# Head sums of batches 4 to 7 on ScalarE's accumulator, exponent clamps of the output weights on GpSimd

## The chip, the cores and the metric

The kernel runs on one core of a Trainium2 chip. A core has a matrix engine (TensorE, PE in the profile, with PEld for its weight loads), VectorE (DVE), ScalarE (ACT), GpSimd (POOL) and SyncE (SP), which here only starts transfers. Each engine takes its own instructions strictly in the order in which the program issues them, and waits at an instruction until its inputs and its output buffer are free. The metric is the device time of one execution in microseconds, as the median of several executions; lower is better.

## The reference

The inputs `q`, `k`, `v` have the shape 8 x 8 x 576 x 64 (batch, head, token, head width) in float32; the three weights arrive as float64. Attention without a softmax gives `x`, and a gated unit with a causal convolution of 5 taps over the tokens gives the output:

```python
kv = np.einsum('bhsd,bhse->bhde', k, v)
out = np.einsum('bhsd,bhde->bhse', q, kv)
rms = np.sqrt(np.mean(out * out, axis=-1, keepdims=True) + 1e-06)
x = out / rms * g_norm            # then (B, S, H*D): 8 x 576 x 512
gate = 1 / (1 + np.exp(-sum over 5 taps of conv_w * shifted x))
result = (gate * (x @ w_val)) @ w_out
```

What matters here is the root mean square: for each token and each head the 64 values of `out` are squared and summed, and the value is then scaled by the sum to the power of -1/2.

## The kernel before

**Order.** The order of the work is written out by hand. `PLAN` (lines 19 to 204) is a list of steps, each a function name with its indices, and lines 816 to 818 call them one after the other. Since each engine works in order, the order of the steps in `PLAN` is the order of every engine's queue, SP's and POOL's transfer queues among them. A step named later can run earlier only if it is on another engine. All eight batches are pipelined against each other: while batch b is normalised, batch b-1 goes through the gate and the value product, and batch pair (b-2)/2 through the output product.

**Batches and chunks.** A batch has 576 tokens, cut into four chunks of 128 tokens (`c` = 0 to 3) and a tail of 64 (`c` = 4). A chunk has 8 heads on 128 partitions; the tail is laid out as 4 head columns on 128 partitions. A step `square 4 1` is chunk 1 of batch 4.

**The path of one chunk, batches 1 to 7.** `raw_pair` (PE) writes the attention output of two chunks into PSUM banks (`raw`, line 501). `square` (ACT, line 535) squares it with two instructions for one chunk, of four heads each, into one of two `sq` buffers in SBUF, whose rows have a 65th column that holds 64 times epsilon. `sums` (DVE, line 544) reduces the 65 columns of each head to `ss`. `powers` (POOL, line 552) raises `ss` to -1/2 and writes `rt`. `normalise` (ACT, line 571) reads `raw` once more and scales it head by head with 8 instructions of 64 columns. `turn_blocks` (DVE) and `move_blocks` (transfers issued by POOL and SP) turn it into `xT`; the tail goes through `turn_x` (PE) and `keep_x` (ACT, line 590).

**What else is in ACT's queue.** `gate_start` (line 615) and `gate_end` (line 628) stand around the four `gate_tap` steps of DVE (line 621). The value product `val_fast` (PE, line 682) writes bank `va`, `vb` or `vc`; `val_keep` with a last index of 0, 1, 2 or 6 (ACT, lines 691, 693, 695, 703) and of 3, 4, 5 (DVE, line 689) copies or adds the bank to `gv`. Indices 0, 2, 4, 6 of `val_fast` all go to the same bank `va`, so `val_fast b m 2` can't start on PE before `val_keep b m 0` has left ACT; index 5 goes to the bank that `val_keep` 1 reads. The output product `fast_product` (PE, line 774) and `fast_keep` (ACT lines 786, 788, 790, 797; DVE line 784) are built in the same way. There are eight PSUM banks, given out in turn. Two lines of `PLAN` show how closely it is woven (the steps on ACT here are `square`, `gate_start`, `val_keep` 0 and 2):

```python
    fast_product 0 3 6; gate_start 3 2; square 4 1; load_q 5 0; load_half k 5 0; square 4 0; turn_blocks 4 2;
    fast_keep 0 3 5; x_sums 3 2; sums 4 0; sums 4 1; val_keep 3 1 0; gate_end 2 3; val_fast 3 1 2; gated 2 3;
```

**The weights.** `narrow_weight` turns float64 into float32 in eight steps per weight piece: step 0 (DVE, line 363) takes the exponent out of the high word into `e`; steps 1, 2 and 3 (ACT, lines 368, 370 and 372) shift it by 896 and clamp it to 0 to 255, place it at bit 23; step 4 (DVE, line 375) adds the sign; steps 5, 6 and 7 (DVE) handle the mantissa and multiply. `wout` has four pieces of 128 x 512, in the order 1, 0, 2, 3.

Of the kernel before, what the change touches and what calls it, by code (L numbers as in the profile page):

```python
# [9 lines left out]
FP32 = mybir.dt.float32  # L10
U32 = mybir.dt.uint32
AF = mybir.ActivationFunctionType
ALU = mybir.AluOpType
AX = mybir.AxisListType

P = 128
EPS = 1e-6
# [190 lines left out]
def kernel(  # L208
# [11 lines left out]
    nc = tc.nc  # L220
    B, H, S, D = q.shape
    C = H * D
    HP = H // 2
    NJ = S // P
# [11 lines left out]
    SV = S // NV  # L236
    ACT_NORM = range(1, B)
    WHOLE = (0,)
    TURNED_X = 2
    FAST_VAL = 2  # L240
    FAST_OUT = 0
# [8 lines left out]
    work = ctx.enter_context(tc.tile_pool(name="work", bufs=2))  # L250
# [18 lines left out]
    wout = const.tile([P, NK, C], FP32, name="wout")  # L269
# [26 lines left out]
    st = {}  # L296
# [51 lines left out]
    def narrow(key, dst, n):  # L348


        w = staged[key]
        rows, size = w.shape[0], w.shape[1]
        split = lambda a: a if len(dst.shape) == 2 else a.rearrange(
            "p (m c) -> p m c", m=dst.shape[1])
        lo, hi = w[:, :, 0], w[:, :, 1]
        if n in (0, 5, 6):
            tag, kind, bufs = {0: ("wexp", U32, 2), 5: ("ot", U32, 3), 6: ("ot", FP32, 3)}[n]
            staged[key, n] = work.tile(
                [P, C], kind, tag=tag, bufs=bufs, name=f"{tag}{n}_{key[0]}{key[1]}")[0:rows, 0:size]
        e, m, mf = (staged.get((key, part)) for part in (0, 5, 6))  # L360

        if n == 0:
            nc.vector.tensor_scalar(
                out=e, in0=hi, scalar1=20, scalar2=0x7FF,
                op0=ALU.logical_shift_right, op1=ALU.bitwise_and,
            )
        elif n == 1:
            nc.scalar.activation(out=e, in_=e, func=AF.Relu, bias=biases[0:rows, 0:1])
        elif n == 2:
            nc.scalar.activation(out=e, in_=e, func=AF.Relu, bias=biases[0:rows, 1:2], scale=-1.0)  # L370
        elif n == 3:
            nc.scalar.activation(
                out=e, in_=e, func=AF.Identity, bias=biases[0:rows, 2:3], scale=-float(1 << 23))
        elif n == 4:
            nc.vector.scalar_tensor_tensor(
                out=e, in0=hi, scalar=0x80000000, in1=e, op0=ALU.bitwise_and, op1=ALU.bitwise_or,
            )
        elif n == 5:

            nc.vector.tensor_scalar(  # L380
                out=m, in0=hi, scalar1=0xFFFFF, scalar2=1 << 20,
                op0=ALU.bitwise_and, op1=ALU.bitwise_or,
            )
        elif n == 6:
            nc.vector.scalar_tensor_tensor(
                out=mf, in0=lo, scalar=2.0 ** -32, in1=m, op0=ALU.mult, op1=ALU.add,
            )
        else:
            nc.vector.scalar_tensor_tensor(
                out=dst, in0=split(mf), scalar=gcol[:] if key[0] == "wval" else 2.0 ** -20,  # L390
                in1=split(e.bitcast(FP32)),
                op0=ALU.mult, op1=ALU.mult,
            )
# [15 lines left out]
    def narrow_weight(*key):  # L409
        narrow(key[0:2], weights[key[0:2]][3], key[2])  # L410
# [34 lines left out]
    def kv_copy(b, s):  # L445
        ps_ = st["kvps", b][s]
        if b in WHOLE:
            for r in range(2):
# [73 lines left out]
    def heads(c):  # L522
        return H if c < NJ else H // 2

    FIRST = {3: 0, 2: H, 4: 2 * H, 1: 2 * H + H // 2, 0: 3 * H + H // 2}

    def square(b, c):
        n = heads(c)
        sq = st["sq", b, c] = sqs[(b * (NJ + 1) + list(FIRST).index(c)) % len(sqs)]
        if b in WHOLE:  # L530
            nc.scalar.activation(  # L531
                out=sq[:, 0:n, 0:D], in_=st["raw", b, c][:].rearrange("p (h e) -> p h e", e=D), func=AF.Square)
            return
        for r, raw in enumerate(st["raw", b, c]):
            nc.scalar.activation(  # L535
                out=sq[:, r * n // 2:(r + 1) * n // 2, 0:D], in_=raw.rearrange("p (h e) -> p h e", e=D),
                func=AF.Square)

    def sums(b, c):
        if ("ss", b) not in st:  # L540
            for name in ("ss", "rt"):
                st[name, b] = work.tile([P, NJ * H + H // 2], FP32, tag=name, bufs=2, name=f"{name}{b}")
        n = heads(c)
        nc.vector.reduce_sum(  # L544
            out=st["ss", b][:, FIRST[c]:FIRST[c] + n], in_=st["sq", b, c][:, 0:n], axis=AX.X)

    def root_range(b, c):
        return slice(FIRST[c], FIRST[c] + ROOTS.get((b, c), heads(c)))

    def powers(b, c):  # L550
        which = root_range(b, c)
        nc.gpsimd.tensor_tensor(  # L552
            out=st["rt", b][:, which], in0=st["ss", b][:, which], in1=mhalf[:, which], op=ALU.pow)

    def normalise(b, c):
# [3 lines left out]
        root = st["rt", b][:, FIRST[c]:FIRST[c] + n]  # L559
        if b in WHOLE:  # L560
            nc.vector.tensor_tensor(
# [240 lines left out]
    def store(i, c, queue=nc.sync, blocks=range(HB)):  # L802
# [5 lines left out]
    steps = {f.__name__: f for f in (  # L808
        load_half, load_q, load_q_rows, stage_weight, narrow_weight, turn_cw, keep_cw, start_warm, warm_up,
        kv_product, kv_copy, turn_q, turn_q_rows, sort_q, raw_whole, raw_pair, raw_tail, square, sums, powers, normalise,  # L810
        turn_x, keep_x, turn_blocks, move_blocks, halo, gate_start, gate_tap, gate_end, val_product, keep_val, gated,
        val_sums, x_sums, val_fast, val_keep, out_product, keep_out, weight_sums, token_sums, fast_product, fast_keep,
# [36 lines left out]
```

## Time and profile before

| What | Value |
|---|---|
| Time, median of 3 runs | 304.34 us (303.98 to 304.76) |
| Span of the profiled execution | 304.6 us |
| PE busy, share of the span | 294.8 us, 97% |
| DVE busy | 269.2 us, 88% |
| ACT busy | 193.7 us, 64% |
| POOL busy | 114.9 us, 38% |

The span is that of one execution, which the page of the profile describes; it agrees with the runs to 0.1%, and no other time is given for this execution. An engine is busy while it executes; matmuls are pipelined, so a busy PE is not PE at its peak. Instructions on ACT overlap at their ends, so the busy time of a group divided by its count is less than the mean duration of one. The timeline of the trace names lines of the kernel; which batch and chunk an instruction belongs to follows by counting, since each line runs in the order of `PLAN`.

### The profile page before, as it was taken

Reading aid. Unit: us, or ns where it says so; the run is one execution under the profiler, and the core shown is the slowest. Engines: PE = TensorE matmul, PEld = TensorE weight load, DVE = VectorE, ACT = ScalarE, POOL = GpSimd, SP = SyncE. Lnnn points to the kernel's source line nnn. Section 1 sums busy time; section 2 is a strip of 40 time slices with the busy share of each in tenths; the row PEclk is TensorE's granted clock in tenths of the full one; section 3 lists DMA queues with packets and bytes.
Section 4 is the critical chain, followed back from the end, with each engine's and each line's share of the span. In section 5 each row is a group of like instructions: output and inputs, shape, how many; then the busy total and the mean of one; then the engine's idle time right before and its main releaser. Section 6 shows DMA issues by size and latency. Waiting matters only on the chain.

```text
span 304.6 us, 8977 instructions
## 1 busy us (share of the span) xinstructions
PE 294.8 (97%) x3441; PEld 232.4 (76%) x3441; DVE 269.2 (88%) x474; ACT 193.7 (64%) x596; POOL 114.9 (38%) x127
## 2 busy tenths in 40 slices
PE   7899999999999999999999999999999999999993
PEld 7788778877787785777778757787878588888582
DVE  1169999999999999999999999999999999999612
ACT  1569989999768664884586547683787354535220
POOL 3027354406568217364338352345536631000000
PEclk9979999999999999999999999999999999999999
DMA  7999998088569756988689477927411621112423
GB/s 269 343 368 343 272 302 210 4 230 269 154 147 329 231 163 167 269 220 260 173 253 294 111 175 232 326 72 214 114 48 30 169 80 34 36 42 64 103 69 103
DMA packets 32074, 55.53 MB, mean 182 GB/s; under 512 B 6166, under 2 KB 14358, under 8 KB 32032
## 3 DMA queue, kind: packets, MB, share of 16 engines
q1 hardware_dynamic: 29520, 49.76, 55.7%
q0 software_dynamic: 1632, 3.17, 4.1%
q10 hardware_dynamic: 880, 2.03, 1.8%
q8 instruction: 27, 0.44, 0.6%
q14 instruction: 15, 0.12, 0.1%
HBM read 39.21 MB, written 9.44 MB: 160 GB/s over the span
## 4 chain that ended last, share of the span: by engine, by line
PE 89%; DVE 5%; DMA 2%; issue 1%; ACT 1%; DVEq 0%; ACTq 0%; SPq 0%
PE a L774 18%; PE cb L774 14%; PE va L682 13%; PE val L633 11%; PE vc L682 6%; PE kvps L440 6%; PE raw L501 5%; PE out L720 5%; PE vb L682 4%; PE qTps L477 4%; PE raw L512 2%; PE xTps L583 2%; DMA qs<-in_q_dram 2%; DVE gate L621 2%; DVE xs L667 1%
## 5 line engine op out<-in xcount | busy, mean ns | idle before, releaser
L552 POOL TENSOR_TENSOR rt<-ss,mhalf 128x8 f32<-128x8 f32 (+3 forms) x38 | 68.9, 1822 | 101.0 <-DVE ss L544 100.8
L621 DVE SCALAR_TENSOR_TENSOR gate<-xT,cwT,gate 128x576 f32<-128x576 f32 x128 | 101.8, 809 | 1.0
L571 ACT ACTIVATE x<-raw,rt 128x64 f32<-128x64 f32 x252 | 55.8, 351 | 7.2 <-POOL rt L552 4.2
L604 POOL DMA_DIRECT2D xT<-y x48 | 26.4, 557 | 25.5 <-DVE ot L784 14.0
L633 PE MATMUL val<-xT,wval 128*128 128x288 f32 x128 | 33.0, 411 | 0.0
L774 PE MATMUL a<-wsum,sums 128*128 128x256 f32 x128 | 32.4, 382 | 0.0
L628 ACT ACTIVATE gate<-gate 128x576 f32<-128x576 f32 x32 | 22.0, 692 | 11.7 <-DVE gate L621 11.4
L633 PEld LDWEIGHTS val<-xT,wval 128*128 128x128 f32 x128 | 23.5, 190 | 6.5 <-ACT xT L590 0.4
L544 DVE TENSOR_REDUCE ss<-sq 128x8 f32<-128x520 f32 (+1 forms) x40 | 24.7, 627 | 2.9 <-ACT sq L531 2.5
L774 PEld LDWEIGHTS a<-wsum,sums 128*128 128x128 f32 x128 | 24.0, 190 | 4.1 <-issue 0.6
L535 ACT ACTIVATE sq<-raw 128x256 f32<-128x256 f32 (+1 forms) x70 | 22.4, 403 | 7.3 <-PE raw L501 7.1
L682 PE MATMUL va<-xs,vsum 128*128 128x288 f32 x96 | 26.6, 409 | 0.0
L615 ACT ACTIVATE gate<-xT,cwT 128x576 f32<-128x576 f32 x32 | 25.2, 811 | 1.5 <-DVE gv L646 1.3
L646 DVE TENSOR_TENSOR gv<-gv,gate 128x576 f32<-128x576 f32 x32 | 23.6, 750 | 0.9 <-ACT gate L628 0.8
L682 PEld LDWEIGHTS va<-xs,vsum 128*128 128x128 f32 x96 | 18.0, 190 | 5.1 <-ACT x L571 0.4
L611 POOL COPY xT<-xT 128x124 f32<-128x124 f32 x32 | 17.5, 585 | 10.5 <-ACT xT L590 10.5
L501 PEld LDWEIGHTS raw<-kv,qT 64*64 64x64 f32 x1008 | 16.4, 134 | 5.3 <-issue 3.0
L440 PEld LDWEIGHTS kvps<-v,k 64*64 64x64 f32 x1008 | 15.9, 135 | 3.7 <-issue 1.9
L501 PE MATMUL raw<-kv,qT 64*64 64x64 f32 x1008 | 18.7, 221 | 0.0
L440 PE MATMUL kvps<-v,k 64*64 64x64 f32 x1008 | 17.6, 220 | 0.0
L774 PE MATMUL cb<-wsum,sums 128*128 128x256 f32 x64 | 16.9, 386 | 0.1
L774 PE MATMUL cb<-wout,gv 128*128 128x256 f32 x64 | 16.8, 385 | 0.0
(111 smaller groups left out, 542.3 us busy)
## 6 DMA issues: line engine op xcount, KB each, us to landing
qs<-in_q_dram SPq DMA_DIRECT2D x96, 140.0 KB, 4.2
out_dram<-ot SPq DMA_DIRECT2D x140, 64.0 KB, 1.7
k<-in_k_dram SPq DMA_DIRECT2D x14, 576.0 KB, 6.3
v<-in_v_dram SPq DMA_DIRECT2D x12, 576.0 KB, 6.5
xT<-y SPq DMA_DIRECT2D x48, 64.0 KB, 2.7
xT<-y POOLq DMA_DIRECT2D x48, 64.0 KB, 3.3
y<-in_moe_w_val_dram SPq DMA_DIRECT2D x4, 512.0 KB, 11.4
w_wout<-in_moe_w_out_dram SPq DMA_DIRECT2D x4, 512.0 KB, 6.3
```

Source lines behind the costliest of these rows:

```text
L440: nc.tensor.matmul(st["kvps", b][s][r * D:(r + 1) * D, i], st["k", b, i][rows, r, cols], st["v", b, i][rows, r, cols], start=(j == 0), sto ...
L501: nc.tensor.matmul(st["raw", b, c][r][cols, to * D:(to + 1) * D], st["qT", b][rows, hp, first:first + D], kvs[b % 2][rows, hp, :], start=T ...
L544: nc.vector.reduce_sum(out=st["ss", b][:, FIRST[c]:FIRST[c] + n], in_=st["sq", b, c][:, 0:n], axis=AX.X)
L552: nc.gpsimd.tensor_tensor(out=st["rt", b][:, which], in0=st["ss", b][:, which], in1=mhalf[:, which], op=ALU.pow)
L571: nc.scalar.activation(out=x[:, to * D:(to + 1) * D], in_=raw[:, h * D:(h + 1) * D], func=AF.Copy, scale=root[:, to:to + 1])
L604: (nc.sync if i % 2 else nc.gpsimd).dma_start(out=xTs[b % 2][i * TB:(i + 1) * TB, :, first:first + P], in_=y[a * TB:(a + 1) * TB, i])
L615: nc.scalar.activation(out=gate[:], in_=xTs[b % 2][:, jt, HALO:SX], func=AF.Copy, scale=cwT[:, K - 1, jt:jt + 1])
L621: nc.vector.scalar_tensor_tensor(out=gate[:], in0=xTs[b % 2][:, jt, tap * TB:tap * TB + S], scalar=cwT[:, tap, jt:jt + 1], in1=gate[:], op ...
L633: nc.tensor.matmul(val[:], wval[:, kc, jt * P:(jt + 1) * P], xTs[b % 2][:, kc, HALO + n * SV:HALO + (n + 1) * SV], start=(kc == 0), stop=( ...
L646: nc.vector.tensor_tensor(out=both, in0=both, in1=st["gate", b, jt][:], op=ALU.mult)
L682: nc.tensor.matmul(st[bank, "val", b, mj][:], weights_[:, k], tokens()[:, k], start=(n in (0, 1, 3) and k == 0), stop=(k == NK // 2 - 1), ...
L774: nc.tensor.matmul(st[bank, i, p], tokens()[:, k], weights_[:, k], start=(n < 2 and k == 0), stop=(k == NK // 2 - 1), skip_group_check=True)
```

## The change

The head sums of batches 4 to 7 (`ACT_SUMS`) are no longer made by DVE. `square` issues one ACT instruction per head instead of one per four heads, and each gives its sum over 64 columns through ScalarE's accumulator output into a column of `ss`. `sums` does nothing for these batches; `powers` has one more GpSimd instruction in front, which adds 64 times epsilon. For the output weights `wout`, steps 1 and 2 of `narrow_weight` are two GpSimd instructions (subtract and clamp below, clamp above and scale), and step 3 is gone. `PLAN` stays as it is.

```diff
+    ACT_SUMS = range(4, B)
...
+        elif key[0] == "wout" and n == 1:
+            nc.gpsimd.tensor_scalar(
+                out=e, in0=e, scalar1=1023.0 - 127.0, scalar2=0.0, op0=ALU.subtract, op1=ALU.max)
+        elif key[0] == "wout" and n == 2:
+            nc.gpsimd.tensor_scalar(
+                out=e, in0=e, scalar1=255.0, scalar2=float(1 << 23), op0=ALU.min, op1=ALU.mult)
+        elif key[0] == "wout" and n == 3:
+            return
...
+    def new_sums(b):
+        for name in ("ss", "rt"):
+            st[name, b] = work.tile([P, NJ * H + H // 2], FP32, tag=name, bufs=2, name=f"{name}{b}")
...
+        if b in ACT_SUMS:
+            if ("ss", b) not in st:
+                new_sums(b)
+            for r, raw in enumerate(st["raw", b, c]):
+                for h in range(n // 2):
+                    to = r * n // 2 + h
+                    nc.scalar.activation(
+                        out=sq[:, to, 0:D], in_=raw[:, h * D:(h + 1) * D], func=AF.Square,
+                        accum_out=st["ss", b][:, FIRST[c] + to:FIRST[c] + to + 1])
+            return
...
     def sums(b, c):
+        if b in ACT_SUMS:
+            return
...
     def powers(b, c):
         which = root_range(b, c)
+        if b in ACT_SUMS:
+            nc.gpsimd.tensor_scalar_add(st["ss", b][:, which], st["ss", b][:, which], D * EPS)
         nc.gpsimd.tensor_tensor(
```

More of the change, by code (lines that the diff above doesn't have):

```diff
@@ L539, in sums @@
     def sums(b, c):
+        if b in ACT_SUMS:
+            return
         if ("ss", b) not in st:
-            for name in ("ss", "rt"):
-                st[name, b] = work.tile([P, NJ * H + H // 2], FP32, tag=name, bufs=2, name=f"{name}{b}")
+            new_sums(b)
         n = heads(c)
```

## The prediction

> **What bounds the kernel now.** I read the page first, its engine shares and the chain of work that ended last:
>
> ```profile
> PE 294.8 (97%) x3441; PEld 232.4 (76%) x3441; DVE 269.2 (88%) x474; ACT 193.7 (64%) x596; POOL 114.9 (38%) x127
> PE 89%; DVE 5%; DMA 2%; issue 1%; ACT 1%; DVEq 0%; ACTq 0%; SPq 0%
> ```
>
> PE carries the chain from 6 us to the end; the 5% of DVE lie between 88 and 107 us, ahead of the first chunk of batch 4. Second, the busy times of the stretch in which batches 4 to 7 are squared and normalised (112 to 245 us; columns: PE, PEld, DVE, ACT, POOL, clock, DMA):
>
> ```profile
> 112.00:145.00 33.00, 32.91 (x408) 24.59 (x407) 32.68 (x55) 20.49 (x72) 17.97 (x24) 1.00 0.81 216
> 145.00:178.00 33.00, 33.00 (x408) 24.58 (x408) 32.83 (x60) 22.48 (x76) 16.70 (x20) 1.00 0.73 208
> 178.00:211.00 33.00, 32.79 (x343) 25.68 (x340) 32.59 (x55) 19.85 (x66) 13.01 (x14) 1.00 0.69 203
> 211.00:245.00 34.00, 33.79 (x346) 25.38 (x345) 32.15 (x53) 23.14 (x78) 18.82 (x21) 1.00 0.38 101
> ```
>
> PE idles 0.5 of 133 us there and DVE 2.75, while ACT idles 47.0: the sums leave the second busiest engine for one at 65%. Whether that is free is decided by ACT's order, so third the timeline of ACT and of PE at one pair of squares (start, duration, line, count, in brackets the idle time before):
>
> ```profile
> 128.63 1.33 ACT L535 ACTIVATE sq<-raw 128x256 f32<-128x256 f32 x4
> 130.30 0.40 ACT L691 COPY gv<-va 128x288 f32<-128x288 f32 x1 [0.34 <-PE va L682]
> 130.60 0.69 ACT L628 ACTIVATE gate<-gate 128x576 f32<-128x576 f32 x1
> 132.14 0.40 ACT L695 COPY gv<-va 128x288 f32<-128x288 f32 x1 [0.85 <-PE va L682]
> ```
> ```profile
> 129.13 1.13 PE L682 MATMUL va<-xT,wval 128*128 128x288 f32 x4
> 130.10 1.03 PE L774 MATMUL a<-wsum,gv 128*128 128x256 f32 x4
> 130.97 1.13 PE L682 MATMUL va<-xs,vsum 128*128 128x288 f32 x4
> ```
>
> After square 4 1 and square 4 0 ACT waits 0.34 us for PE, copies bank va until 130.70 (val_keep 3 1 0), and at 130.97 PE writes that same bank again (val_fast 3 1 2). So ACT has 0.34 + 0.27 us to spare here; whatever the squares take beyond it stops PE, which is in order and, being at full rate, never catches up. Last, durations by shape (count, busy us, mean ns):
>
> ```profile
> L535 ACT ACTIVATE sq<-raw 128x256 f32<-128x256 f32 x56 | 19.0, 428 | 6.1 <-PE raw L501 5.9
> L535 ACT ACTIVATE sq<-raw 128x128 f32<-128x128 f32 x14 | 3.4, 302 | 1.2 <-PE raw L501 1.2
> L294 ACT ACTIVATE warm<-warm 128x1 f32<-128x1 f32 x1 | 0.2, 203 | 0.0
> L552 POOL TENSOR_TENSOR rt<-ss,mhalf 128x8 f32<-128x8 f32 x29 | 55.0, 1901 | 89.8 <-DVE ss L544 89.6
> ```
>
> **Removed: 20 reductions on DVE.** By shape, line 544's 40 instructions take 0.685 us with 8 heads and 0.396 for a tail, so 16 x 0.685 + 4 x 0.396 = 12.5 us leave DVE. They buy almost nothing. PE idles 0.5 us from 112 to 245, and the chain is PE from there to the end; DVE merely keeps up. Between 0.5 and 1 us is the most that can come back.
>
> **Added: 144 head squares on ACT instead of 40 squares.** A batch has 4 x 8 + 4 = 36 heads. From 428 and 302 ns at 256 and 128 columns (126 ns for 128 columns) 64 columns take 239 ns. Four squares of 256 last 1.33 us, so three steps take 0.90, 0.30 each, and neighbours overlap by 0.13. How the accumulator is written out no row shows. Low bound: free, 0.239 - 0.13 = 0.11 us a head. High bound: a second instruction with one element per partition, as the 203 ns row, with no overlap at all: 0.44. I take 0.31: the second instruction exists and can't start before the last square is summed, but the next square overlaps with it (0.239 + 0.203 - 0.13). It is also near the middle of the bounds. By the Trainium skill, page "ScalarE: Activation LUTs", section on what a table load costs, an ACTIVATE with immediates takes 186 ns + 0.833 ns a column and neighbours overlap by 93 ns: an estimate of 0.146 for 64 columns and no price for the accumulator; the sum by it would be 306 us with a free accumulator, against 304.4 by the rows.
>
> A chunk took 2 x 0.339 = 0.68 us (19.0 / 56) and now takes 8 x 0.31 = 2.48: +1.80. A tail took 0.49 (3.4 / 14, twice) and takes 1.24: +0.75. Over four batches 16 x 1.80 + 4 x 0.75 = 31.8 us more on ACT, whose load from 112 to 245 rises from 86 to 118 of 133 us.
>
> What of it reaches PE, place by place (times of the trace before; "slack" is from the end of an ACT instruction to the PE instruction that needs it; "carried" is how far ACT lags behind an already delayed PE):
> - 118.6, squares 4 3 and 4 2: +3.6. ACT idles 1.89 before keep_x 3 4; val_keep 3 0 0 has 0.44 slack. Stall 1.3.
> - 128.6, 4 1 and 4 0: 0.44 carried + 3.6 - 0.34 - 0.27 = 3.4.
> - 142.0, 4 4: +0.75 under 2.4 idle: 0.
> - 150.0, 5 2 and 5 3: 3.6 - 0.5 idle - 1.09 slack (val_keep 4 0 0) = 2.0.
> - 157.6, 5 0 and 5 1: 1.09 carried + 3.6 - 0.28 - 1.34 slack (val_keep 4 0 1) = 3.1.
> - 170.0, 5 4: under 1.7 idle: 0.
> - 184.0 and 188.3, 6 3 and 6 2: 1.8 - 1.4 (val_keep 5 1 0) = 0.4, then 1.8 - 0.55 + 1.8 - 0.24 (val_keep 5 0 1) - 0.4 = 2.4.
> - 195.1, 6 1: gate_end 4 3 behind it is waited for by gated 4 3, token_sums 2 0 0 and fast_product 2 0 1, with 0.1 slack: 1.7.
> - 201.2, 6 0: 2.1 slack (fast_keep 2 1 2): 0.
> - 213.9, 6 4: kv_copy 7 1 has 0.38 slack: 0.4.
> - 216.7, 7 3 and 7 2: 3.6 - 0.53 (fast_keep 1 3 0) = 3.1.
> - 223.4 and 226.1, 7 0 and 7 1: 3.6 - 1.45 idle - 1.65 slack (val_keep 6 1 2) = 0.5.
> - 238.0, 7 4: under 4.5 idle: 0.
>
> Sum 1.3 + 3.4 + 2.0 + 3.1 + 2.8 + 1.7 + 0.4 + 3.1 + 0.5 = 18.3 us. The same walk with 0.44 a head (+2.84 a chunk, +1.27 a tail) gives 3.4 + 5.5 + 4.1 + 5.2 + 4.9 + 2.7 + 0.7 + 0.9 + 5.2 + 2.6 = 35; with 0.21 about 7; with 0.11 (+0.2 a chunk) 0.1.
>
> **Added: 20 epsilon adds on POOL.** The power takes 1901 ns for 8 columns and 1205 for 4: 174 ns a column and 0.5 fixed. The add lies between 0.1 (a 128x1 MEMSET on POOL, 98 to 115 ns) and 1.2; I take the fixed 0.5, the nearest row with the same shape. It takes the place of a 0.69 us reduction between square and power: even, 0. At 1.2 it would be 0.5 longer, and ACT waits for rt five times from 112 to 245: at most +2.5. Behind the adds in POOL's queue stand move_blocks and halo; the one place close in time is halo 4 at 162.3, and x of a batch is moved some 10 us ahead of its first x_sums.
>
> **Moved: the clamp of wout.** ACT loses 12 instructions, 3.1 + 3.1 + 2.9 = 9.1 us, between 38 and 70 us. PE runs at full rate there, so this buys 0 to 0.3. POOL gains 8 instructions of 512 columns. Nearest rows: the 128x128 AFFINE_SELECT at 292 ns, the 124-column halo copy at 585 ns. Bounds 0.3 (no dearer than the select) and 2.4 (585 x 512 / 124); I take 1.2 (292 x 4, contiguous as here). POOL's idle time before the next power is 7.85 us at piece 1, 2.54 and 3.07 at piece 0, 10.61 at pieces 2 and 3: all fit, and step 4 on DVE comes 5.4 us or more after step 0 for every piece. At 2.4 each, powers 1 3 and 2 3 start 1.1 late: +1.0 at most. I take 0.
>
> Against this part speaks the Trainium skill, page "SBUF — State Buffer", section "Who interferes with whom": a DVE instruction with two SBUF inputs contends with a GpSimd instruction that reads SBUF, and the one that issues second blocks. In this trace gate_tap (two SBUF inputs) takes 0.807 us alone, 0.807 under a power, and 0.831 under halo's copies: 3%, no full block. By the rows 8 x 1.2 us of clamps cost DVE 0.3 us, by the rule up to 9.6, which the DVE stretch at 88 to 107 us would hand to PE: 332 us.
>
> Sum: 304.34 + 18.3 = 322.6 us (the span of 304.6 on which the sum rests is 0.1% above the median of the runs).
>
> **The rivals.**
> - *ACT has the room* (ends on the other side). If a head costs 0.12 us or less, the squares stay within the slack, PE is untouched, and at most 1 us comes back from DVE and 0.3 from the clamp: 303 to 304.5. For it: ACT idles 47 us in the stretch, and an accumulator could be written by the instruction itself. Against: 0.12 is under the 0.20 step of the existing 64-column ACTs of line 571 (8 in 1.75 us). It decides where 16 heads take less than the 1.36 us of two chunks now plus 0.6. Chance 0.08: 0.05 faster, 0.03 no change.
> - *A cheap accumulator*: 0.15 to 0.25 a head, the existing step of line 571 and little more. 306 to 312 us. Chance 0.25.
> - *The accumulator read stands alone*: nothing overlaps, 0.38 to 0.44 a head, 329 to 340 us. For it: a sum must be complete before it is read, and it must be read before the next one begins. Against: every ACT pair in the trace overlaps. Chance 0.20.
> - *Clamps block DVE* as above: forecast plus up to 10 us, 325 to 332. Against it the 3%. Chance 0.07.
> - My forecast, 0.25 to 0.38 a head, 312 to 329 us. Chance 0.40.
>
> **How the numbers follow.** 322.6 is the likeliest. The range must leave out 2 in 10: the first rival and the lowest part of the second fall below 309, the upper end takes in the third: 309 to 340. The kernel's runs differ by 0.13% from their median, so 0.3% (0.9 us) is about what tells a change from none: faster 0.05, same 0.03, slower 0.92.
>
> **What would show it.** Line 535 would have 144 instructions of 64 columns and about 240 ns, with a second ACT instruction of about 200 ns each or not; ACT's busy time would rise by 32 - 9 = 23 us, to about 216. PE's idle time from 118 us on would be released by ACT at lines 691, 693, 695, 786 and 788 and be near 18 us, the longest by squares 4 1 and 4 0 and 7 3 and 7 2. DVE would fall to about 257 us. The stretch to 112 us would end within 1 us of before. What would make me wrong: another price of a head (each 0.1 us is worth about 13 us), taps longer under the clamps, or a lag of DVE through gate_start and gate_end that I count only once.

## The result and the profile after

The changed kernel takes 313.48 us (median, 312.94 to 314.22) against 304.21 us before: 9.3 us more, a ratio of 1.0295 with a 95% interval of 1.0268 to 1.0322. The forecast of slower was right and the range of 309 to 340 holds the time, but the predicted 18.3 us were twice what came.

One thing about the times first. The profiled execution of after has a span of 311.6 us and a time of 313.66: about 2 us lie around a span, and the spans and times of the runs below show the same. The span of 304.6 us of before is therefore not typical. In it the granted clock was 0.79 from 16 to 24 us, and PE stood 2.4 us later at 35 us than in the profile of the changed kernel, and 2.5 to 2.7 us later than in eight of the twelve profiles below. By the same 2 us its own time would be some 306.6 (an estimate), above all four runs of before here (303.98 to 304.76). The statement in the prediction that it agrees with the median to 0.1% compared a span with a time. The forecast was a difference added to the median, so it did not suffer from this. Comparisons of spans would, and below I compare how lags grow within a trace instead.

The page of after, engine shares and chain:

```profile
PE 293.7 (94%) x3441; PEld 229.9 (74%) x3441; DVE 262.4 (84%) x454; ACT 203.8 (65%) x832; POOL 142.2 (46%) x155
PE 55%; ACT 13%; DVE 13%; DMA 7%; POOL 7%; issue 3%; SPq 1%; ACTq 0%; DVEq 0%; POOLq 0%
```

PE has fallen from 89% of the chain to 55%; mainly ACT, DVE, POOL and transfers took its place. ACT is only 10 us busier in all (about +19 for the squares, -9 for the clamps). The stretch of batches 4 to 7 (columns: PE, PEld, DVE, ACT, POOL, clock, DMA):

```profile
112.00:145.00 33.00, 31.21 (x401) 23.17 (x400) 29.35 (x50) 25.07 (x132) 19.77 (x25) 1.00 0.73 214
145.00:178.00 33.00, 31.61 (x392) 24.80 (x394) 27.97 (x49) 24.50 (x134) 18.35 (x24) 1.00 0.66 194
178.00:211.00 33.00, 31.91 (x275) 23.45 (x267) 29.29 (x49) 24.59 (x124) 14.02 (x18) 1.00 0.66 190
211.00:245.00 34.00, 32.26 (x419) 25.80 (x418) 27.92 (x46) 27.71 (x145) 17.89 (x23) 1.00 0.37 97
```

PE now idles 6.0 of 133 us instead of 0.5, DVE 18.5 instead of 2.75, while ACT still has 31 us idle. No engine is full; they wait for each other. How one head looks on ACT, from the timeline (start, duration):

```profile
119.11 0.22 ACT L553 ACTIVATE sq<-raw 128x64 f32<-128x64 f32 x1 [0.81 <-PE raw L510]
119.23 0.19 ACT L553 ACTIVATION_READ_ACCUMULATOR sq<-raw 128x1 f32 x1
119.32 0.22 ACT L553 ACTIVATE sq<-raw 128x64 f32<-128x64 f32 x1
119.43 0.20 ACT L553 ACTIVATION_READ_ACCUMULATOR sq<-raw 128x1 f32 x1
```

The accumulator read is an instruction of its own, as I had taken it to be, but it starts 0.1 us after its square, under its tail, and the next square starts 0.1 us after that: 0.20 us a head, not 0.31. The place that the prediction showed, the bank copy behind squares 4 1 and 4 0 on ACT, and PE there:

```profile
132.80 0.58 ACT L717 COPY gv<-va 128x288 f32<-128x288 f32 x1
```
```profile
130.61 1.03 PE L800 MATMUL a<-wsum,gv 128*128 128x256 f32 x4
133.43 1.24 PE L708 MATMUL va<-xs,vsum 128*128 128x288 f32 x4 [1.79 <-ACT gv L717]
```

PE waits 1.79 us for the copy, in the very place that was named. The clamps (line 369 and 372) and the epsilon add (line 577), by shape on POOL:

```profile
L372 POOL TENSOR_SCALAR wexp_wout<-wexp_wout 128x512 uint32<-128x512 uint32 x4 | 8.9, 2227 | 0.3
L369 POOL TENSOR_SCALAR wexp_wout<-wexp_wout 128x512 uint32<-128x512 uint32 x4 | 8.7, 2176 | 7.6 <-DVE wexp_wout L364 7.6
L577 POOL TENSOR_SCALAR ss<-ss 128x8 f32<-128x8 f32 x16 | 6.2, 388 | 36.6 <-ACT sq L553 36.2
```

A clamp takes 2.2 us, near the upper bound of 2.4 and not the 1.2 taken; the add takes 0.39, near the 0.5 taken.

Where the time went is seen by setting the start of each of PE's 3441 weight loads, which come in the same order in both kernels, against the same load of before. The lag of after stands at -2.4 us from 28 to 36 us (the clock of before). It grows by 0.66 near 38 us, 0.71 near 62 and 1.50 near 78, stands at 0.55 from 80 to 128 us, and grows to 6.98 us by 220 us, after which it does not change. So 2.9 us were lost ahead of the first square of batch 4, and 6.4 us behind it. Of the 0.66 near 38 us, 0.24 also stands in six of the kernels below that left the clamps on ScalarE, and so is not the clamps'.

### The profile page after: what moved, and what is told of

Same layout as the page of the kernel before. It is cut to its first block, busy times and chain, and to the rows that moved or that the text cites. A ratio compares the mean times of both kernels' runs of the same rounds, so it can differ in the third digit from the quotient of the medians.

```text
span 311.6 us, 9218 instructions
## 1 busy us (share of the span) xinstructions
PE 293.7 (94%) x3441; PEld 229.9 (74%) x3441; DVE 262.4 (84%) x454; ACT 203.8 (65%) x832; POOL 142.2 (46%) x155
## 4 chain that ended last, share of the span: by engine, by line
PE 55%; ACT 13%; DVE 13%; DMA 7%; POOL 7%; issue 3%; SPq 1%; ACTq 0%; DVEq 0%; POOLq 0%
PE a L800 15%; PE cb L800 11%; PE va L708 10%; ACT sq L553 6%; PE vc L708 5%; POOL rt L578 5%; DVE gate L647 4%; PE kvps L449 4%; PE out L746 3%; ACT x L597 3%; DMA v<-in_v_dram 3%; PE raw L510 3%; PE vb L708 3%; DMA qs<-in_q_dram 2%; DMA out_dram<-ot 2%
## 5 line engine op out<-in xcount | busy, mean ns | idle before, releaser
L647 DVE SCALAR_TENSOR_TENSOR gate<-xT,cwT,gate 128x576 f32<-128x576 f32 x128 | 103.1, 821 | 4.5 <-ACT gate L641 3.4
L597 ACT ACTIVATE x<-raw,rt 128x64 f32<-128x64 f32 x252 | 57.0, 382 | 9.6 <-POOL rt L578 7.5
L553 ACT ACTIVATE sq<-raw 128x64 f32<-128x64 f32 x144 | 30.7, 319 | 3.9 <-PE raw L510 3.9
L654 ACT ACTIVATE gate<-gate 128x576 f32<-128x576 f32 x32 | 23.1, 726 | 11.0 <-DVE gate L647 11.0
L553 ACT ACTIVATION_READ_ACCUMULATOR sq<-raw 128x1 f32 x144 | 30.3, 305 | 0.0
L577 POOL TENSOR_SCALAR ss<-ss 128x8 f32<-128x8 f32 (+1 forms) x20 | 7.8, 392 | 42.5 <-ACT sq L553 42.0
L637 POOL COPY xT<-xT 128x124 f32<-128x124 f32 x32 | 18.5, 617 | 11.3 <-ACT xT L616 11.3
```

The costliest lines, as they stand in the source:

```text
L553: nc.scalar.activation(out=sq[:, to, 0:D], in_=raw[:, h * D:(h + 1) * D], func=AF.Square, accum_out=st["ss", b][:, FIRST[c] + to:FIRST[c] ...
L597: nc.scalar.activation(out=x[:, to * D:(to + 1) * D], in_=raw[:, h * D:(h + 1) * D], func=AF.Copy, scale=root[:, to:to + 1])
L647: nc.vector.scalar_tensor_tensor(out=gate[:], in0=xTs[b % 2][:, jt, tap * TB:tap * TB + S], scalar=cwT[:, tap, jt:jt + 1], in1=gate[:], op ...
```

## The experiments

Three sets of four kernels were run, each set on one chip together with before. Differences are of medians; the ratio stands with its 95% interval.

**One part alone: the head sums.**

```diff
-        elif key[0] == "wout" and n == 1:   (and n == 2, n == 3: the GpSimd branches)
```

> Only the head sums of batches 4 to 7 move to ScalarE; the clamps of wout stay on ScalarE as before. Theory 1 (the squares delay ScalarE's bank copies and account for what was lost after 112 us, the clamps for the rest): about +6.4 us. Rival (the clamps cost nothing, the two profiled executions merely began differently): +9.3 us, the whole loss. My walk with the measured 0.20 us a head: +6.

Measured 310.84 against 304.80, +6.0 us, ratio 1.0199 (1.0162 to 1.0235). From 40 to 112 us PE's lag does not move (-2.3 to -2.2); then it grows by 6.5 us at the same places and by the same amounts as in the changed kernel. PE's waits from 112 to 250 us in this kernel (engine, line waited at, who was waited for, total, times, longest):

```profile
PE vc L700 <- ACT gv L711: 1.8, 2, 1.3
PE va L700 <- ACT gv L709: 1.8, 1, 1.8
PE a L792 <- ACT ot L804: 1.5, 1, 1.5
PE va L700 <- issue: 0.5, 2, 0.3
PE vc L700 <- ACT ot L746: 0.3, 1, 0.3
```

All but the issue pauses are for bank copies on ACT. Theory 1 holds.

**One part alone: the clamps.**

```diff
-    ACT_SUMS = range(4, B)
+    ACT_SUMS = ()
```

> Only the clamps of wout move to GpSimd. Theory 1: +2 to +3 us, lost between 36 and 80 us, where TensorE's lag grew by 0.66, 0.71 and 1.50 us. Rival: within 0.3 us of before, as the prediction had it.

Measured 307.06 against 304.80, +2.3 us, ratio 1.0068 (1.0044 to 1.0091). The lag grows by 0.65, 0.72 and 1.50 us where it did in the changed kernel, and not after 82 us. The two parts come to 2.0% and 0.7%, against 2.95% (2.68 to 3.22) for both; by PE's lag they are 6.5 and 2.9 of 9.4 us. The clamps, which I had put at nothing, are a quarter of the loss.

**What a head costs without the accumulator.**

```diff
+        if b >= 4:      # one Square per head, no accum_out; sums stay on VectorE
+            for r, raw in enumerate(st["raw", b, c]):
+                for h in range(n // 2):
+                    nc.scalar.activation(out=sq[:, r * n // 2 + h, 0:D], in_=raw[:, h * D:(h + 1) * D], func=AF.Square)
+            return
```

> Batches 4 to 7 are squared head by head on ScalarE, but without the accumulator; VectorE sums as before. This separates the price of 64-column instructions from that of the accumulator read. If the read takes its own 0.10 us step of the 0.20: a chunk takes 8 x 0.10 to 0.11, +0.2 us against before, and the time stays within 0.3 us of before. If the 64-column instruction itself takes 0.20 and the read hides behind it: the loss of the change after 112 us, about +6 us.

Measured 305.64 against 304.80, +0.8 us, ratio 1.0031 (1.0009 to 1.0053). The timeline of ACT at squares 4 1 and 4 0:

```profile
127.20 2.05 ACT L537 ACTIVATE sq<-raw 128x64 f32<-128x64 f32 x16
128.88 0.67 ACT L697 COPY gv<-va 128x288 f32<-128x288 f32 x1
```

Sixteen squares from 127.20 to 128.88 are 0.105 us each. So the step of 0.20 is half square, half read, and the read is what makes the change dear: without it 36 heads a batch cost about 1 us in all over four batches, with it 6. The +0.8 is more than the 0.3 expected and is not traced further; PE's lag grows by 1.3 us in steps of 0.1 to 0.4 us.

**What VectorE's relief is worth.**

```diff
+    ssone = const.tile([P, NJ * H + H // 2], FP32, name="ssone")     # ones
     def sums(b, c):
+        if b >= 4:  st["ss", b] = ssone; return
```

> Batches 4 to 7 are squared as before, but nobody sums them: the power reads a constant tile of ones, so the root mean square of these batches is left out, and the powers no longer wait for the squares. This is the most that VectorE's relief can give. Theory 1 (TensorE is the bound): between -1 and 0 us against before. Rival (VectorE's 12.5 us were worth something): more than 1 us faster.

Measured 303.33 against 304.80, -1.5 us, ratio 0.9952 (0.9931 to 0.9974). In the trace PE gains 1.1 us on before between 124 and 204 us. The rest of the 1.5 is within what the interval leaves open (0.8 to 2.1 us). By the letter of the expectation this is the rival's side, more than 1 us, if narrowly. My bound of "between 0.5 and 1 us" was slightly low, and reductions of 12.5 us taken off an engine that was 98% busy are worth about a tenth of that, as PE sets the pace.

**Only where it was free.** Ten of the twenty chunks, chosen from the lag of the changed kernel.

```diff
+    ACT_SUMS = {(4, 3), (4, 2), (4, 4), (5, 4), (6, 1), (6, 0), (6, 4), (7, 0), (7, 1), (7, 4)}
-        if b in ACT_SUMS:
+        if (b, c) in ACT_SUMS:
```

> ScalarE sums only ten of the twenty chunks of batches 4 to 7: those behind which TensorE lost nothing in the changed kernel (4 3, 4 2, 4 4, 5 4, 6 1, 6 0, 6 4, 7 0, 7 1, 7 4); the clamps stay on ScalarE. Theory (only squares right ahead of a tight bank copy cost): no loss, and up to 1 us gained from VectorE's relief: -1 to +0.3 us. Rival (every chunk costs by its load on ScalarE): about half of what all twenty cost, +3 us.

Measured 304.92 against 304.46, ratio 1.0012 (0.9981 to 1.0043): no difference. Four of the ten chunks are tails, so these are 64 of the 144 heads; by load they would cost some 2.7 of the 6.0 us. They cost nothing that can be measured, so the loss is not by load alone. The one wait for compute that is left on PE between 112 and 250 us is this:

```profile
196.38 1.13 PE L792 MATMUL cb<-wsum,sums 128*128 128x256 f32 x4 [0.87 <-DVE sums L770]
```

It is the place that the prediction named for square 6 1: gate_end 4 3 stands behind it on ACT, and gated 4 3, token_sums 2 0 0 and fast_product 2 0 1 follow one after the other on DVE and PE. The walk with 0.20 a head gives 0.8. In the changed kernel PE does not wait there; it already runs 5.3 us late.

**The same without chunk 6 1.**

```diff
-    ... (6, 1), (6, 0), ...
+    ... (6, 0), ...
```

> As the run with ten chunks, but without chunk 6 1, whose squares stand ahead of gate_end 4 3 and which kept VectorE's token sums and TensorE waiting 0.87 us at 196 us: nine chunks on ScalarE's accumulator, the clamps on ScalarE. Theory (place decides): 0.5 to 1 us less than the run with ten chunks, so -0.7 to 0 us against before. Rival (load): as the run with ten chunks, less a tenth.

Measured 304.16 against 304.55, ratio 0.9980 (0.9957 to 1.0003); the wait at token_sums is gone. It is the fastest version that computes everything, but it can't be told from before.

**The other half, moved.** All twenty chunks, with four steps put behind the copies that they delayed.

```diff
-square 4 1; square 4 0; ... val_keep 3 1 0; gate_end 2 3;
+square 4 1; ... val_keep 3 1 0; square 4 0; gate_end 2 3;
-square 5 1; ... val_keep 4 0 1;
+val_keep 4 0 1; square 5 1;
-square 6 2; val_keep 5 0 1; ... val_keep 5 1 2;
+val_keep 5 0 1; ... val_keep 5 1 2; square 6 2;
-square 7 2; ... powers 7 2; gate_start 5 3; keep_x 6 4;
+gate_start 5 3; keep_x 6 4; square 7 2; powers 7 2;
```

> All twenty chunks are summed on ScalarE and the clamps stay on ScalarE, but four steps go to another place in the order: square 4 0 behind val_keep 3 1 0, square 5 1 behind val_keep 4 0 1, square 6 2 behind val_keep 5 1 2, and square 7 2 with powers 7 2 behind keep_x 6 4. Theory (the order before the bank copies costs, not the load): about 0.5 us is left at each of the four places, so +1 to +2.5 us instead of +6. Rival (the load of 19 us more on ScalarE costs): +5 to +6 us, wherever the squares stand.

Measured 310.31 against 304.46, +5.8 us, ratio 1.0184 (1.0130 to 1.0237): the rival was right. The four waits did shrink, from 1.79, 1.33, 0.50 and 1.53 us to 0.15, 0.66, 0 and 0. But others came:

```profile
PE cb L792 <- DVE sums L770: 1.5, 1, 1.5
PE va L700 <- ACT gv L709: 0.8, 2, 0.7
PE vc L700 <- ACT x L589: 0.6, 1, 0.6
```

**Moved further.** Square 4 0 behind gate_start 3 0, square 6 1 behind gate_end 4 3, the rest as in the run before.

```diff
-val_keep 3 1 0; square 4 0; ... gate_start 3 0;
+val_keep 3 1 0; ... gate_start 3 0; square 4 0;
-square 6 1; gate_end 4 3;
+gate_end 4 3; square 6 1;
```

> All twenty chunks on ScalarE, clamps on ScalarE, moved as in the run before, but square 4 0 further back, behind gate_start 3 0, and also square 6 1 behind gate_end 4 3. The run before left +5.8 us: its waits had gone to other places (1.5 us at token_sums behind gate_end 4 3, 0.3 behind val_keep 3 1 2, 0.24 behind val_keep 3 0 4). Theory (place decides): these three go, and +2.5 to +4 us are left. Rival (the load of 19 us comes back at some other place whatever is moved): +5 to +6 us.

Measured 310.47 against 304.55, +5.9 us, ratio 1.0181 (1.0146 to 1.0216). The rival again. The 1.5 us at token_sums 2 0 0 are gone, and two others came up: 0.93 us at another token sum,

```profile
143.53 1.10 PE L792 MATMUL cb<-wsum,sums 128*128 128x256 f32 x4 [0.93 <-DVE sums L770]
```

and 0.3 at a normalise. In the profiles PE's lag behind 112 us grows by 6.5 us with nothing moved, 6.3 with the first moves and 5.4 with these. What DVE waits for from 112 to 250 us has grown too, but not by the moves. Before:

```profile
DVE gv L646 <- ACT gate L628: 0.8, 2, 0.6
```

with the head sums alone, nothing moved:

```profile
DVE gv L664 <- ACT gate L646: 7.6, 5, 2.4
DVE gate L639 <- ACT gate L633: 3.1, 2, 2.4
```

and in this kernel:

```profile
DVE gv L664 <- ACT gate L646: 6.4, 7, 1.6
DVE gate L639 <- ACT gate L633: 1.7, 3, 0.7
```

DVE, which was as full as PE, waits for gate_end as soon as all twenty chunks are summed on ACT, and the moves spread these waits over more places (7 instead of 5) without taking them away. That they are what keeps the moved kernels slow is not shown. The theory that the place decides holds for nine of the ten chunks behind which PE had lost nothing (6 1 leaves a wait of 0.87 us) and for no more; the other ten had no free place among those tried. Whether a whole new order would find one is open.

**Clamps: queue or held VectorE.** The clamps alone had two suspects: theory Q, that a power waits behind clamps of 2.2 us in POOL's queue, and theory D, that DVE is held while a clamp reads. Both are seen in the run with the clamps alone. DVE's fused step that starts 0.15 us after the first clamp takes 1.09 us instead of 0.68, and the powers 2 3 stand behind the clamps of piece 3 until 68.6:

```profile
35.28 1.09 DVE L394 SCALAR_TENSOR_TENSOR ot_wval<-y,ot_wval 128x512 f32<-128x512 uint32 x1
37.68 1.16 DVE L647 SCALAR_TENSOR_TENSOR gate<-xT,cwT,gate 128x576 f32<-128x576 f32 x1
```
```profile
64.22 2.04 POOL L369 TENSOR_SCALAR wexp_wout<-wexp_wout 128x512 uint32<-128x512 uint32 x1 [3.03 <-DVE wexp_wout L364]
66.34 2.27 POOL L372 TENSOR_SCALAR wexp_wout<-wexp_wout 128x512 uint32<-128x512 uint32 x1
```

Seven DVE instructions between 30 and 72 us are 0.24 to 0.41 us longer than others of their shape, 2.5 us in all; in before there is none. With the head sums alone the powers 2 3 start at 66.21, here at 68.69.

Most of that delay is not the queue's. The sum that the powers 2 3 need is the first of these two:

```profile
67.76 1.28 DVE L568 TENSOR_REDUCE ss<-sq 128x8 f32<-128x520 f32 x2
```

It ends at 68.44, the second clamp at 68.61, so the queue holds this power back by some 0.2 us. The sum itself is 2.38 us later than with the head sums alone. Setting each DVE instruction against the same one of that kernel shows why: DVE's lag grows by 2.55 us from 35 to 68 us, in seven steps, one behind each lengthened instruction, and DVE waits for nothing in between. By this trace theory D makes nearly all of the delay. Without the holds the two clamps, behind a step 0 that ends at 62.5 us, would have been done at about 67.0 (an estimate), 0.8 us past the 66.2 of the head sums alone; so Q stands behind D at the same place.

The first test took the powers out from behind the clamps.

```diff
-narrow_weight wout 3 0; ... narrow_weight wout 3 1; narrow_weight wout 3 2;   (piece 3, ahead of powers 2 3)
+... narrow_weight wout 2 2; narrow_weight wout 3 1; narrow_weight wout 3 2;   (step 0 behind wout 0 7)
-narrow_weight wout 0 2; narrow_weight wout 0 4;
+powers 1 1; narrow_weight wout 0 2; ... turn_q 2 2; narrow_weight wout 0 4;
```

> Only the clamps of wout move to GpSimd, and they are placed where no power waits behind them: those of piece 3 directly behind those of piece 2, with its step 0 earlier on VectorE, the second clamp of piece 0 behind powers 1 1, and step 4 of piece 0 a little later. Theory Q (the powers queue behind clamps of 2.2 us): the losses of 0.66 and 1.5 us vanish and +0.4 to +0.8 us are left of 2.3. Theory D (each clamp holds VectorE for 0.35 to 0.4 us, 3 us in all): +2 us or more as before, since VectorE is held as often.

Measured 307.57 against 304.46, ratio 1.0110 (1.0077 to 1.0142): +3.1 us, not less than the clamps in their old places. Against Q alone; but the powers 2 3 now waited 1.2 us for a sum on DVE, whose steps I had moved too, so the test was not clean. DVE was also held less often than theory D supposed, at four places instead of seven, 1.4 us in all.

The second kept the clamps on ScalarE and only occupied POOL.

```diff
+            if key[0] == "wout":      # step 1; step 2 the same without the copy
+                nc.gpsimd.tensor_copy(idle[:, 0:1], e[:, 0:1])
+                for _ in range(4): nc.gpsimd.memset(idle[:], 0.0)
```

> The clamps of wout stay on ScalarE. In their places GpSimd fills a tile that nobody reads, four times 512 columns for each clamp (about 2 us), after reading one column of the exponents, so that it starts no earlier than a clamp would: the same occupation of GpSimd's queue, without reads of SBUF. Theory Q: +1.5 to +2.3 us. Theory D: within 0.5 us of before, and no VectorE instruction is lengthened by 0.35 us.

Measured 307.59 against 304.46, ratio 1.0091 (1.0053 to 1.0129). An occupied POOL is enough to cost 3 us; 1.8 of PE's lag came from 41 to 48 us, where the clamps had cost nothing, and 1.4 behind powers 2 3. But ScalarE waited 0.9 us for POOL's reading of the exponents, and two DVE instructions were still lengthened, by 0.24 and 0.42. So, once more with the copy reading step 5's tile, which ScalarE does not touch:

```diff
-                nc.gpsimd.tensor_copy(idle[:, 0:1], e[:, 0:1])
+                if key[1] != 0: nc.gpsimd.tensor_copy(idle[:, 0:1], m[:, 0:1])
```

> The clamps of wout stay on ScalarE. In their places GpSimd fills an unused tile, 2.27 us for each clamp as in the fill before, but its start now hangs on step 5 of VectorE (piece 0: on nothing), so that no step of ScalarE has to wait for it. Theory Q (powers queue behind what GpSimd does for wout): +1.5 to +3 us, with ScalarE waiting for rt. Theory D (VectorE is held): within 0.5 us, since no reads of SBUF are left.

Measured 309.97 against 304.55, ratio 1.0195 (1.0138 to 1.0252). That is more than either theory gives, and the trace shows why it must not be taken whole:

```profile
37.03 1.97 PE L510 MATMUL raw<-kv,qT 64*64 64x64 f32 x59 [2.52 <-issue]
79.03 0.47 PE L510 MATMUL raw<-kv,qT 64*64 64x64 f32 x14 [0.97 <-ACT gv L651]
80.94 1.13 PE L783 MATMUL cb<-wout,gv 128*128 128x256 f32 x4 [0.37 <-ACT ot L797]
```

About 4 us are lost from 34 to 41 us: PE pauses for 2.5 us in the middle of one product, waiting for nothing that the profile shows, and behind the pause the granted clock is 0.72 from 36 to 38 us, 0.50 from 38 to 40 and 0.92 from 40 to 42. The third loss of the clamps, that behind powers 2 3, comes back with 1.8 us (1.5 with the clamps), and only one DVE instruction is lengthened in this run, by 0.17 us at 40 us. At 60 us nothing is lost. Here the sum that powers 2 3 need ends at 69.36 and the power starts at 71.55, behind the fills. So a full queue can make the third loss by itself; with the clamps the same gap was 68.44 to 68.69.

The last test shortened the clamps to 64 columns.

```diff
-                out=e, in0=e, scalar1=1023.0 - 127.0, ...
+                out=e[:, 0:64], in0=e[:, 0:64], scalar1=1023.0 - 127.0, ...      (the same for step 2)
```

> Only the clamps of wout move to GpSimd, and each takes only the first 64 of 512 columns, so that the rest of the exponents is not clamped and the output weights are not the reference's: as many GpSimd instructions and holds of VectorE as in the change, but a queue that is free again after some 0.4 us. Theory Q: within 0.5 us of before. Theory D: +1.5 to +2.3 us, as for the whole clamps.

Measured 304.29 against 304.55, ratio 0.9991 (0.9967 to 1.0014): the loss is gone. As many instructions of 0.69 us cost nothing; it is the 2.2 us that count. It does not tell the theories apart, though, since not one DVE instruction is lengthened here either. For D speak, beside the late sum of powers 2 3, the first loss (PE waits 0.39 us for a DVE weight step two steps behind the first lengthened one, which was held 0.41 us) and the second, at 60 us, where powers 1 1 started 1.2 us later than with the head sums alone because sums 1 1 on DVE was 1.2 us later; where POOL only writes, that loss is 0.2 us or none. So with the clamps all three losses follow DVE's lag, by the trace. This is not tested by a kernel with holds and without queueing, and how much the queue adds is open.

## Why the prediction was right or wrong

- **That the squares would stop PE through the bank copies behind them:** right, shown by the head sums alone (+6.0 of 9.3 us) and the waits at the copies of val_keep and fast_keep.
- **The price of a head, 0.31 us:** the term that was mis-sized; it measured 0.20. I let the read begin only after the square had ended and gave one overlap of 0.13; in truth both steps overlap. The bounds of 0.11 and 0.44 held it. A row of the trace was nearer than the one I used: the 64-column normalise with its step of 0.20. By it the rival "cheap accumulator" (306 to 312 us, chance 0.25) was the case that came for this part: 310.8. That this row fits so well is partly luck: a bare square of the same 64 columns has a step of 0.105.
- **The walk by places:** right about where. The same walk with 0.20, so +0.91 a chunk, against how much PE's lag grew in the changed kernel:

| Place (us of before) | Forecast at 0.31 | Walk at 0.20 | Measured |
|---|---|---|---|
| 118.6, 4 3 and 4 2 | 1.3 | 0 | 0 |
| 128.6, 4 1 and 4 0 | 3.4 | 1.2 | 2.1 |
| 150.0, 5 2 and 5 3 | 2.0 | 0.2 | 0.6 |
| 157.6, 5 0 and 5 1 | 3.1 | 1.3 | 1.6 |
| 184 to 188, 6 3 and 6 2 | 2.8 | 1.0 | 1.3 |
| 195.1, 6 1 | 1.7 | 0.8 | 0 (0.87 where nothing else is late) |
| 213.9, 6 4 | 0.4 | 0 | 0 |
| 216.7, 7 3 and 7 2 | 3.1 | 1.3 | 1.8 |
| 223.4, 7 0 and 7 1 | 0.5 | 0 | 0 |
| 142 to 150 | 0 | 0 | -0.6 |
| Sum | 18.3 | 5.8 | 6.8; 6.4 with smaller gains |

  Place by place the walk at 0.20 is 0.3 to 0.9 us short at five places and 0.8 over at 6 1, and it leaves out the gain of 0.6, so its sum is nearer than its terms. At 4 1 and 4 0 0.4 us more came from normalise 4 2, which waited for rt on POOL (0.37 us), a delay that I had set to even.
- **Relief of DVE, at most 0.5 to 1 us:** nearly right; 1.1 us in the trace of the kernel without sums, 1.5 by the clock. What shows as -0.6 at 142 to 150 us in the table is part of it.
- **The epsilon add, 0.5 us taken, counted as even:** 0.39 measured. It left ACT waiting for rt a little longer, as above.
- **The clamps, taken as 0 with an upper end of +1.0:** wrong. They cost 2.3 us. The step that failed is the 0.3 us by which they were to lengthen DVE, and which the sum left out: I had scaled the 3% of halo's copies, but the holds sum to 2.5 us, and DVE, which had no idle time there, passed all of it on, so that the sum for powers 2 3 came 2.4 us late. "All fit" failed as well: the exponents of piece 3 are there only 3.7 us ahead of the power (64.75 against 68.45 in before), whatever POOL's idle time, and two clamps take 4.4. The delay by the queue for which I had a bound of 1.1 us is about 0.8 by the estimate above; the power's whole delay was 2.5. The page "SBUF — State Buffer" of the Trainium skill, section "Who interferes with whom", has it that a DVE instruction with two SBUF inputs and a GpSimd instruction that reads SBUF contend. The trace agrees that they do and not that the second is blocked throughout: the hold is 0.24 to 0.41 us at seven places, in clamps of 2.2 us, though each held instruction started after its clamp. The rival of blocked DVE named the right mechanism at a quarter of its price (2.5 of up to 9.6 us). "Taps longer under the clamps" stood among what would make me wrong, and four of the seven held instructions are taps.
- **What would show it:** 144 squares with a second instruction each, as said. ACT's busy time rose by 10 and not 23 us, DVE fell to 262.4 and not 257: with the head sums alone it is 259.9, since DVE instructions overlap at their ends and 12.5 us of durations are 9.3 of busy time, and the holds add 2.5. PE's waits lie, but for 0.3 us, at lines 717, 719 and 812 (691, 693 and 786 of before), the longest at 4 1 and 4 0 and at 7 3 and 7 2, as said; they are 6 and not 18 us. "The stretch to 112 us would end within 1 us of before" was wrong by the clamps.

## What to carry to other kernels

In a kernel whose engines all follow one order written by hand, idle time of an engine is not room: price each added instruction by the slack of the first instruction behind it that another engine waits for, and take that walk through the trace with the lowest and the highest price. Here, with the measured price put in afterwards, it was good to a microsecond at each place, and it gives 0 for each of the nine chunks whose head sums then cost nothing. For an unmeasured pair of instructions, carry the steps of the short instructions on that engine (here 0.20 for the nearest) as well as full durations through the sum. Check a "fits into the idle time" claim at the upper end of the price, from the moment the input is there, and ask what the moved work does to an engine that has no idle time.

## What the runs showed of the hardware

- ScalarE's accumulator output is a second instruction, ACTIVATION_READ_ACCUMULATOR, and costs 0.09 to 0.10 us of step behind a square of 64 columns, whose own step is 0.105 us.
- A GpSimd tensor_scalar with two operations on uint32 takes 2.2 us for 512 columns and 0.69 for 64: about 3.4 ns a column and 0.47 us fixed; with one operation on 8 float columns 0.39 us.
- Each GpSimd clamp of 512 columns (2.2 us) lengthened at most one VectorE instruction, by 0.24 to 0.41 us in seven cases of eight, one that started 0.15 to 0.63 us after the clamp; those of 64 columns (0.69 us) lengthened none. VectorE, without idle time there, ran later by the sum of these holds.
- In one kernel PE paused for 2.5 us in the middle of a product without waiting for anything that the profile shows. Behind it the granted clock fell to 0.50 (38 to 40 us), and both together cost 4 us; why PE paused is open.
